# An attention and mixture-of-experts kernel: the expert stage's DMAs put in a fixed order per queue

## The chip, the cores and the metric

The kernel runs on one core of one Trainium2 chip. The metric is the device time of one launch in microseconds. The kernel before took 986.78 us, the median of 3 runs.

## What is computed

The reference is a chain of three layers on 3072 tokens of 384 numbers.

```python
# 1: linear attention with decay (batch 4, heads 8, sequence 768, head size 48)
state = alpha[:, :, t, :, None] * state + einsum('bhd,bhe->bhde', k[:, :, t], v[:, :, t])
y[:, :, t] = einsum('bhd,bhde->bhe', q[:, :, t], state)
# 2: a gated block (384 -> 1024 -> 1024 -> 384)
x = ((x @ w1) * (x @ w2) @ w3) @ w_out
# 3: 8 experts (384 -> 1024 -> 384), each token goes to the two with the largest logits
noisy_logits = x @ w_gate + log1p(exp(x @ w_noise)) * noise
out[mask] += top2_w * (maximum(x[mask] @ w1[e], 0) @ w2[e])
```

The change is in the third layer, the expert stage.

## The kernel before

**The stages.** Attention and the gated block run interleaved on TensorE until expert 0's first layer; the gated block's last products come last. The tokens go in 8 groups of 384 (three tiles of 128 rows). When the last narrow product of a group is done, `finish` (L566) scales its rows, cuts them into a high and a low float16 half ("xr") and stores them to a table of rows in device memory, "x2s" (L583). `route` (L607) then works out the two experts and the two factors of each token on VectorE. `rank` (L650) counts, with a product on TensorE of the 0/1 matrix "M" (L657), the place that each token gets in its experts' lists, and GpSimd writes number and factor there, six scattered writes a group (L686) into "table". The groups' rankings go one after another; the last one, `rank(NG - 1)`, comes inside expert 0's second layers.

**One expert.** An expert takes up to 832 tokens in two parts, 512 and 320 (the list `PARTS`, L949); what is over goes to a loop at the end (`overflow`). For a part, `fetch_part(e, p)` (L955) does three things: SP loads the part's slots from "table" into "mt" (`slots`, L939), and GpSimd gathers the rows of each 128 tokens from "x2s" into "xg" (`gather`, L883). `turn_part` (L963) then has SP transpose an "xg" into its place in "xT" by a DMA (`turn`, L890). Expert 0's and 1's first parts hold only tokens of the first six groups, so they don't need the last two rankings; their second parts need them. `first(e, p, f)` (L967, `layer1` L893) is one of eight steps of the first layer: nine matmuls (L897 to L899) into one bank, ScalarE's relu to "hh" (L900) and VectorE's rest "hl" (L901). `second(e, p, t)` (L973, `layer2` L903) makes 24 matmuls (L907 to L909) for 128 tokens, ScalarE scales the result into "ysb" (L930), and GpSimd adds it to the output by an indirect DMA (L931). The last 64 tokens of a part of 320 go through `last_few` (L981).

**The weights.** `expert_weights` (L826) and `weight_steps` (L840) give a list of small steps for each of the two matrices. A matrix is loaded in two halves, each by one DMA of SP into one of three buffers "es" (L853). VectorE takes each half's largest absolute value (L856), then "em", the larger of both for each partition (L859); TensorE's one-column product `over_all` takes it over the partitions (L864); five small steps make a scale of it (L868 to L872, "esc"); then ScalarE and VectorE cut the half into a high and a low float16 part, "eh" and "el" (L181 and L185, in `split`). A buffer is free for the next load when its half is cut. Below, the matrices are a (first) and b (second) and their halves a0, a1, b0 and b1.

**What sets the order.** These steps wait in a list, `todo`. `prepare(n)` (L1008) takes n of them, after a first, a second layer or a narrow product; the list `EARLY` says how many are taken behind each of the last narrow products. TensorE runs in the order of the code. The other engines' instructions are placed by a scheduler, which may move them past each other where no data forbids it and `tc.issue_after` does not say otherwise. SP's and GpSimd's DMAs are among these: each engine issues its own in the order in which they stand, and one that has to wait holds up what stands behind it.

```python
1022    def experts():
1023        leave(ST2)
1024        weights_for(1)
1025        fetch_part(1, 0)
1026        for f in range(NF):
1027            first(0, 0, f)
```

In the loop over the experts 1 to 7 (from L1058 on) TensorE's order is: first layer of part 0, first layer of part 1, four second layers of part 0, three of part 1. Expert 1's first layer of part 0 stands ahead of expert 0's of part 1.

Of the kernel before, what the change touches and what calls it, by code (L numbers as in the profile page):

```python
# [20 lines left out]
P = 128  # L21
# [3 lines left out]
E = 8  # L25
# [31 lines left out]
Q1 = 1  # L57
Q2 = 3
Q3 = 1
Q4 = 1  # L60
ST1 = 15
ST2 = 9
EARLY = (3, 3, 3, 3, 0, 0, 1, 0, 1, 0, 1, 0, 1, 0, 0, 0, 0, 0, 2, 0, 0, 0, 1, 1, 1, 1)
T1 = 1
# [21 lines left out]
def body(ctx, tc, q, k, v, alpha, mw1, mw2, mw3, mwo, wg, wn, noise, ew1, ew2, out, dbg=None):  # L86
# [564 lines left out]
    def rank(g):  # L651
# [32 lines left out]
        for j in range(2):  # L684
            for t in range(TG):
                i = nc.gpsimd.indirect_dma_start(  # L686
                    out=table_rows, out_offset=bass.IndirectOffsetOnAxis(ap=ad[:, j, t:t + 1], axis=0),
                    in_=md[:, j, t, :], in_offset=None)
# [134 lines left out]
    ep = None  # L823

    def expert_weights(e):
# [10 lines left out]
        if isinstance(e, int) and e == 0:  # L836
            return r, a[:2] + b[:1] + a[2:4] + b[2:3] + a[5:10] + b[1:2] + a[10:] + b[3:4] + b[5:]
        return r, a[:2] + b[:1] + a[2:-NK] + b[1:2] + a[-NK:] + b[2:]

    def weight_steps(src, e, n, m, hi, lo, sc):  # L840
# [8 lines left out]
        def get(i):  # L849
# [3 lines left out]
            nc.sync.dma_start(s[i], half(w, i))  # L853
# [29 lines left out]
    def gather(mt, t, rows=NTOK + P):  # L883
        xg = ep.tile([P, 2 * DM], F16, name="xg", bufs=7)
        nc.gpsimd.indirect_dma_start(  # L885
            out=xg, out_offset=None, in_=x2s[:rows],
            in_offset=bass.IndirectOffsetOnAxis(ap=mt[:, t, 0:1].bitcast(U32), axis=0))
        return xg

    def turn(xg, xT, t):  # L890
        nc.sync.dma_start_transpose(out=xT[:, :, t * P:(t + 1) * P], in_=xg)
# [36 lines left out]
    def put(py, n, mt, wv, t, e=None):  # L928
        ys = ep.tile([P, DM], F32, name="ysb", bufs=3)
        nc.scalar.activation(ys[:n], py, AF.Copy, scale=wv[:n, t:t + 1])  # L930
        i = nc.gpsimd.indirect_dma_start(  # L931
            out=out, out_offset=bass.IndirectOffsetOnAxis(ap=mt[:n, t, 0:1].bitcast(U32), axis=0),
            in_=ys[:n], in_offset=None, compute_op=OP.add)
# [85 lines left out]
    def leave(n):  # L1019
        prepare(max(0, len(todo) - n))  # L1020

    def experts():
        leave(ST2)
        weights_for(1)
        fetch_part(1, 0)
        for f in range(NF):
            first(0, 0, f)
            prepare(Q1)
        leave(ST1 + ST2)
        for t in range(NTP[0]):  # L1030
            turn_part(1, 0, t)
            second(0, 0, t)
            prepare(Q2)
            if t == 0:
                rank(NG - 1)
        fetch_part(0, 1)
        fetch_part(1, 1)
        leave(ST2)
        for f in range(NF):
            first(1, 0, f)  # L1040
            prepare(Q3)
            if 0 <= f - NF + NTP[1] + T1 < NTP[1]:
                turn_part(0, 1, f - NF + NTP[1] + T1)
        for f in range(NF):
            first(0, 1, f)
            prepare(Q4)
        leave(0)
        weights_for(2)
# [177 lines left out]
```

## Time and profile before

| | |
|---|---|
| median of 3 runs | 986.78 us (986.07 to 995.55) |
| the profiled execution | 993.42 us |
| its span | 991.7 us |
| mean granted clock of TensorE in it | 0.969 of full |
| TensorE, VectorE, ScalarE and GpSimd busy | 94, 62, 46 and 26% of the span |

All times of the trace are from the profiled execution, and count from the start of its span. A timeline row gives the start and the length of an instruction or a run of like ones, its engine, line and operation, what it writes and reads, how many they are (x), and in brackets the idle time of the engine before it with what ended that. L numbers are lines of the kernel before. Engines are PE (TensorE), PEld (its weight loads), DVE (VectorE), ACT (ScalarE), POOL (GpSimd) and SP; SPq is SP issuing a DMA. A windows row gives the busy time of PE, PEld, DVE, ACT and POOL in this order, each with its count of instructions, then the granted clock, the share of the DMA engines' time and the bytes moved.

### The profile page before, as it was taken

What the parts mean: (1) busy time and instruction counts of PE and PEld (TensorE: products, weight loads), DVE (VectorE), ACT (ScalarE), POOL (GpSimd) and SP (SyncE); (2) the same over time, 40 slices, a digit from 0 to 9 for tenths busy, and PEclk for the clock granted to TensorE, in tenths of its full rate; (3) what the DMA queues carried; (4) which work ended last, traced back from release to release, by engine and by line L of the source; (5) the groups of instructions that cost most, each with busy time, mean ns of one, the idle gap of its engine ahead of it and who ended that gap; (6) DMA issues with size and microseconds to landing.
All of it is one profiled execution on the core that took longest, in us unless ns stands there. A gap on an engine that the chain in (4) does not pass through costs nothing.

```text
span 991.7 us, 17686 instructions
## 1 busy us (share of the span) xinstructions
PE 927.8 (94%) x6823; PEld 607.9 (61%) x6823; DVE 615.6 (62%) x1697; ACT 457.6 (46%) x916; POOL 253.4 (26%) x246
## 2 busy tenths in 40 slices
PE   7889999999899998999979898999899999999996
PEld 4777777777566665766635454655456555655564
DVE  6698878676689696886657756525355453635220
ACT  3876764363555656555535342434233332433321
POOL 2121110004031403022222162333241424242313
PEclk9798999999999999999989998999899999999999
DMA  9895681406615033001051358567566475657203
GB/s 248 217 164 99 164 216 32 93 12 208 120 30 84 9 73 49 25 1 46 13 179 45 119 145 192 100 136 145 118 138 143 106 157 122 159 128 132 37 9 45
DMA packets 189269, 105.54 MB, mean 106 GB/s; under 512 B 156912, under 2 KB 174912, under 8 KB 189184
## 3 DMA queue, kind: packets, MB, share of 16 engines
q1 hardware_dynamic: 172624, 68.04, 30.7%
q0 software_dynamic: 16560, 36.37, 16.7%
q8 instruction: 54, 0.88, 0.4%
q14 instruction: 31, 0.25, 0.1%
HBM read 73.06 MB, written 20.31 MB: 94 GB/s over the span
## 4 chain that ended last, share of the span: by engine, by line
PE 55%; DVE 20%; issue 8%; ACT 7%; DMA 6%; SPq 3%; POOL 0%; POOLq 0%; ACTq 0%; DVEq 0%
PE ps L907 5%; PE ps L908 5%; PE ps L909 5%; PE ps L897 4%; PE ps L899 4%; PE ps L898 4%; DVE esc L856 3%; DMA es<-in_moe_w_dram 3%; PE ps L532 3%; PE ps L534 3%; PE ps L533 3%; PE ps L556 2%; PE ps L558 2%; PE ps L557 2%; PE ps L350 2%
## 5 line engine op out<-in xcount | busy, mean ns | idle before, releaser
L931 POOL DMA_INDIRECT out_dram<-ysb,mt x56 | 87.7, 1567 | 243.4 <-ACT ysb L930 141.0
L901 DVE SCALAR_TENSOR_TENSOR hl<-ps,hh 128x512 f16<-128x512 f32 (+1 forms) x128 | 74.4, 586 | 107.6 <-ACT hh L900 77.2
L897 PE MATMUL ps<-xT,eh 128*128 128x320 f16 (+1 forms) x384 | 131.9, 344 | 4.0 <-DMA xT<-xg 4.0
L898 PE MATMUL ps<-xT,eh 128*128 128x320 f16 (+1 forms) x384 | 132.2, 344 | 0.0
L899 PE MATMUL ps<-xT,el 128*128 128x320 f16 (+1 forms) x384 | 132.0, 344 | 0.0
L908 PE MATMUL ps<-el,hh 128*128 128x384 f16 x384 | 126.2, 329 | 0.0
L907 PE MATMUL ps<-eh,hh 128*128 128x384 f16 x384 | 126.1, 328 | 0.0
L909 PE MATMUL ps<-eh,hl 128*128 128x384 f16 x384 | 126.0, 328 | 0.0
L900 ACT ACTIVATE hh<-ps 128x512 f16<-128x512 f32 (+1 forms) x128 | 65.7, 515 | 110.4 <-PE ps L899 93.7
L930 ACT ACTIVATE ysb<-ps,wv 128x384 f32<-128x384 f32 (+1 forms) x56 | 32.4, 579 | 149.9 <-PE ps L909 103.4
L185 DVE SCALAR_TENSOR_TENSOR el<-es,esc,eh 128x512 f16<-128x512 f32 (+1 forms) x80 | 66.8, 855 | 46.6 <-ACT eh L181 41.4
L686 POOL DMA_INDIRECT table<-md,ad x48 | 49.5, 1031 | 147.9 <-DVE ad L683 102.8
L856 DVE TENSOR_REDUCE esc<-es 128x1 f32<-128x1536 f32 x32 | 55.9, 1746 | 38.8 <-DMA es<-in_moe_w_dram 35.2
L885 POOL DMA_INDIRECT xg<-x2s,mt x56 | 56.3, 1006 | 54.9 <-DMA mt<-table 32.1
L183 POOL TENSOR_TENSOR sm<-sf,sm 128x512 f16<-128x512 f32 x24 | 28.4, 1200 | 163.4 <-ACT sm L181 163.3
L532 PE MATMUL ps<-xT,w1h 128*128 128x384 f16 (+2 forms) x204 | 66.2, 325 | 2.0 <-ACT ab L536 1.6
L536 ACT ACTIVATE ab<-ps 128x384 f32<-128x384 f32 (+2 forms) x136 | 61.1, 465 | 14.9 <-PE ps L534 13.8
L556 PE MATMUL ps<-Wh,gh 128*128 128x400 f16 x192 | 64.8, 337 | 2.9 <-ACT gh L181 1.5
L181 ACT ACTIVATE eh<-es,esc 128x512 f16<-128x512 f32 (+1 forms) x80 | 61.9, 797 | 11.5 <-DVE esc L871 11.5
L534 PE MATMUL ps<-xT,w1l 128*128 128x384 f16 (+2 forms) x204 | 66.4, 326 | 0.0
L533 PE MATMUL ps<-xT,w1h 128*128 128x384 f16 (+2 forms) x204 | 66.4, 326 | 0.0
L532 PE MATMUL ps<-xT,w0h 128*128 128x384 f16 (+2 forms) x204 | 65.1, 320 | 1.1 <-ACT xT L403 1.1
(285 smaller groups left out, 2091.9 us busy)
## 6 DMA issues: line engine op xcount, KB each, us to landing
es<-in_moe_w_dram SPq DMA_DIRECT2D x32, 768.0 KB
s<-in_moe_w_dram POOLq DMA_DIRECT2D x16, 512.0 KB
out_dram<-zero POOLq DMA_DIRECT2D x5, 960.0 KB
v<-in_v_dram SPq DMA_DIRECT2D x24, 192.0 KB
x2s<-xr SPq DMA_DIRECT2D x24, 192.0 KB
pad<-in_alpha_dram SPq DMA_DIRECT2D x21, 192.0 KB
pad<-in_q_dram SPq DMA_DIRECT2D x21, 192.0 KB
pad<-in_k_dram SPq DMA_DIRECT2D x21, 192.0 KB
```

Source lines behind the costliest of these rows:

```text
L532: nc.tensor.matmul(pm, wab[i][0][:, kk, fs], xT[:, kk, cs], start=kk == 0, stop=False)
L533: nc.tensor.matmul(pm, wab[i][0][:, kk, fs], xT[:, NK + kk, cs], start=False, stop=False)
L534: nc.tensor.matmul(pm, wab[i][1][:, kk, fs], xT[:, kk, cs], start=False, stop=kk == NK - 1)
L556: nc.tensor.matmul(pm, gh[:, ts], Wf[0][:, f], start=f == 0, stop=False)
L856: nc.vector.tensor_reduce(sc[:, 5 + i:6 + i], s[i], AX.XY, OP.max, apply_absolute_value=True)
L897: nc.tensor.matmul(pm, w1h[:, kk, fs], xT[:, kk, :n], start=kk == 0, stop=False)
L898: nc.tensor.matmul(pm, w1h[:, kk, fs], xT[:, NK + kk, :n], start=False, stop=False)
L899: nc.tensor.matmul(pm, w1l[:, kk, fs], xT[:, kk, :n], start=False, stop=kk == NK - 1)
L907: nc.tensor.matmul(py[:n], hh[:, f, ts], w2h[:, f], start=f == 0, stop=False)
L908: nc.tensor.matmul(py[:n], hh[:, f, ts], w2l[:, f], start=False, stop=False)
L909: nc.tensor.matmul(py[:n], hl[:, f, ts], w2h[:, f], start=False, stop=f == NF - 1)
L931: i = nc.gpsimd.indirect_dma_start(out=out, out_offset=bass.IndirectOffsetOnAxis(ap=mt[:n, t, 0:1].bitcast(U32), axis=0), in_=ys[:n], in_o ...
```

## The change

All DMAs of the expert stage are made through a new function, `queued`, which holds each behind the one made last on either queue (SP's and GpSimd's): the order of the code is now the order of the queues. (Table writes are bound so only for the last group; in the overflow loop `line` is None and nothing is bound.) The code's order is changed with it. An expert's first three weight loads (a0, a1, b0) are made as soon as its list is opened, ahead of its slots; `next_weights(e + 2)` opens it behind the second layers of part 0 of expert e, where before it was opened at the start of expert e + 1. Its other steps are spaced by empty ones (`pause`), and both maxima of b stand next to each other. Expert 0's three loads stand ahead of the slot loads of expert 0 and 1. `rank(NG - 1)` moves from behind expert 0's first second layer to in front of it, and the slots and gathers of expert 0's second part from behind the four second layers to behind the first of them. In experts 2 to 7 the second part's slots are fetched ahead of the second layers of the expert before, and its transposes stand in these. There are three buffers for the slots of each part (two before) and eight for gathered rows (seven before).

```diff
-EARLY = (3, 3, 3, 3, 0, 0, 1, 0, 1, ...
+EARLY = (0, 3, 0, 3, 2, 1, 0, 1, 0, 1, ...
...
-                i = nc.gpsimd.indirect_dma_start(
+                i = queued(lambda: nc.gpsimd.indirect_dma_start(
                     out=table_rows, out_offset=bass.IndirectOffsetOnAxis(ap=ad[:, j, t:t + 1], axis=0),
-                    in_=md[:, j, t, :], in_offset=None)
+                    in_=md[:, j, t, :], in_offset=None), g > NG - NL)
...
+    line = {}
+
+    def queued(dma, on=True):
+
+        if not on or line is None:
+            return dma()
+        with ExitStack() as st:
+            for d in line.values():
+                st.enter_context(tc.issue_after(d))
+            d = dma()
+        line[d.ins.engine] = d.ins
+        return d
...
-        if isinstance(e, int) and e == 0:
-            return r, a[:2] + b[:1] + a[2:4] + b[2:3] + a[5:10] + b[1:2] + a[10:] + b[3:4] + b[5:]
-        return r, a[:2] + b[:1] + a[2:-NK] + b[1:2] + a[-NK:] + b[2:]
+        return r, a, b
...
-            nc.sync.dma_start(s[i], half(w, i))
+            queued(lambda: nc.sync.dma_start(s[i], half(w, i)))
...
-        xg = ep.tile([P, 2 * DM], F16, name="xg", bufs=7)
+        xg = ep.tile([P, 2 * DM], F16, name="xg", bufs=8)
...
-        mt = ep.tile([P, NTA, 2], F32, name=f"mt{part}")
-        nc.sync.dma_start(mt[:, :n], src)
+        mt = ep.tile([P, NTA, 2], F32, name=f"mt{part}", bufs=3)
+        queued(lambda: nc.sync.dma_start(mt[:, :n], src))
...
-        weights_for(0)
-    def begin_experts():
-        fetch_part(0, 0)
+        a, b = weights_for(0)
+        todo.extend(a[2:4] + b[2:3] + a[5:10] + b[1:2] + a[10:] + b[3:4] + b[5:])
+        for e in range(NFR):
+            fetch_part(e, 0)
...
     def weights_for(e):
-        EW[e], st = expert_weights(e)
-        todo.extend(st)
+        EW[e], a, b = expert_weights(e)
+        for get in a[:2] + b[:1]:
+            get()
+        return a, b
+    def pause(n):
+        return [lambda: None] * n
+    def next_weights(e):
+        a, b = weights_for(e)
+        todo.extend(pause(1) + a[2:4] + pause(1) + a[5:10] + b[1:2] + a[10:] + pause(1) + b[2:4] + pause(2) + b[5:])
...
     def experts():
-        leave(ST2)
-        weights_for(1)
-        fetch_part(1, 0)
+        prepare(len(todo))
+        a, b = weights_for(1)
+        todo.extend(pause(1) + a[2:4] + pause(1) + a[5:11] + b[1:2] + a[11:] + b[2:3] + pause(2) + b[3:4] + pause(1) + b[5:])
         for f in range(NF):
             first(0, 0, f)
-            prepare(Q1)
-        leave(ST1 + ST2)
+            prepare(1)
+        rank(NG - 1)
         for t in range(NTP[0]):
             turn_part(1, 0, t)
             second(0, 0, t)
-            prepare(Q2)
+            prepare(3)
             if t == 0:
-                rank(NG - 1)
-        fetch_part(0, 1)
-        fetch_part(1, 1)
-        leave(ST2)
+                fetch_part(0, 1)
         for f in range(NF):
             first(1, 0, f)
-            prepare(Q3)
-            if 0 <= f - NF + NTP[1] + T1 < NTP[1]:
-                turn_part(0, 1, f - NF + NTP[1] + T1)
+            prepare(1)
+            if 0 < f <= NTP[1]:
+                turn_part(0, 1, f - 1)
+        prepare(len(todo))
+        fetch_part(1, 1)
+        next_weights(2)
         for f in range(NF):
             first(0, 1, f)
-            prepare(Q4)
-        leave(0)
-        weights_for(2)
+            prepare(f // 4)
...
         for e in range(1, E):
-            if 1 < e < E - 1:
-                weights_for(e + 1)
             if e > 1:
-                fetch_part(e, 1)
...
-                    if 3 <= f < 3 + NTP[1]:
-                        turn_part(e, 1, f - 3)
             if e + 1 < E:
                 fetch_part(e + 1, 0)
...
+            if e + 1 < E:
+                fetch_part(e + 1, 1)
             for t in range(NTP[0]):
                 second(e, 0, t)
                 prepare(2)
                 if e + 1 < E:
                     turn_part(e + 1, 0, t)
             prepare(len(todo))
+            if e + 2 < E:
+                next_weights(e + 2)
             if e < E - 1:
                 for t in range(NTP[1] - 1):
+                    turn_part(e + 1, 1, t)
                     second(e, 1, t)
+                turn_part(e + 1, 1, NTP[1] - 1)
                 rest = last_few(e)
...
-        begin_experts()
```

In the three places below, rows of the two kernels' instruction orders are shown. A row is one instruction, or several in a row (x); L numbers are lines of the kernel it belongs to, those of the changed one being up to 10 larger or smaller than those given above, and a number in a tile's name tells buffers apart.

SP's DMAs around expert 0's first loads, before. "mt_6556" holds the slots of expert 0's first part; "es" of 3x512 is a half of a, of 4x384 a half of b.

```order
L853 DMA es<-in_moe_w_dram 128x3x512
L941 DMA mt_6556<-table 128x8
L853 DMA es<-in_moe_w_dram 128x3x512
L853 DMA es<-in_moe_w_dram 128x4x384
L891 DMA_TRANSPOSE xT_6558<-xg 128x6x128 x4
L853 DMA es<-in_moe_w_dram 128x4x384
```

The same place in the changed kernel ("mt_6562" and "mt_6573" hold the slots of expert 0's and 1's first parts, "xr" the rows of the last group):

```order
L856 DMA es<-in_moe_w_dram 128x3x512 x2
L856 DMA es<-in_moe_w_dram 128x4x384
L944 DMA mt_6562<-table 128x8
L944 DMA mt_6573<-table 128x8
L576 DMA x2s<-xr 128x768 x3
L856 DMA es<-in_moe_w_dram 128x4x384
L894 DMA_TRANSPOSE xT_6564<-xg 128x6x128 x4
```

Before, the second and third loads stood behind the slot load; now three loads stand in front of it, and expert 1's slot load behind it.

SP's DMAs beside expert 0's second layers and expert 1's first layer, before ("xT_7207" is expert 1's first part, "mt_7499" and "xT_7501" expert 0's second part, "mt_7508" the slots of expert 1's second part):

```order
L891 DMA_TRANSPOSE xT_7207<-xg 128x6x128 x4
L853 DMA es<-in_moe_w_dram 128x4x384
L941 DMA mt_7499<-table 128x6
L941 DMA mt_7508<-table 128x6
L853 DMA es<-in_moe_w_dram 128x3x512
L891 DMA_TRANSPOSE xT_7501<-xg 128x6x128 x3
```

The same place in the changed kernel ("xT_6575" is expert 1's first part, "mt_7397" and "xT_7399" expert 0's second part, "mt_7617" the slots of expert 1's second part):

```order
L894 DMA_TRANSPOSE xT_6575<-xg 128x6x128
L856 DMA es<-in_moe_w_dram 128x4x384
L944 DMA mt_7397<-table 128x6
L894 DMA_TRANSPOSE xT_6575<-xg 128x6x128 x3
L894 DMA_TRANSPOSE xT_7399<-xg 128x6x128 x3
L944 DMA mt_7617<-table 128x6
```

Three of the four transposes for expert 1's first layer now stand behind the slot load of expert 0's second part, which reads what the last ranking wrote.

VectorE beside expert 0's first layer, before. "hl" is that layer's own work, one row a step; "esc" and "em" are expert 1's maxima; L626 to L635 are the last group's routing.

```order
L901 SCALAR_TENSOR_TENSOR hl_7217<-ps,hh_7216 128x512
L629 TENSOR_REDUCE rr<-ln 128x3
L856 TENSOR_REDUCE esc_7199<-es 128x1
L630 TENSOR_TENSOR oh<-rev,rr 128x24
L901 SCALAR_TENSOR_TENSOR hl_7217<-ps,hh_7216 128x512
L632 SCALAR_TENSOR_TENSOR nl<-oh,nl 128x24
L856 TENSOR_REDUCE esc_7199<-es 128x1
L626 TENSOR_REDUCE m<-nl 128x3
L901 SCALAR_TENSOR_TENSOR hl_7217<-ps,hh_7216 128x512
L627 TENSOR_TENSOR ln<-nl,m 128x24
L635 TENSOR_TENSOR w<-m 128x3
L859 TENSOR_REDUCE em<-esc_7199 128x1
```

The same layer in the changed kernel, from its second step on (L178 is the cut of the last group's third tile of rows, L590 to L593 an earlier part of the routing):

```order
L904 SCALAR_TENSOR_TENSOR hl_7223<-ps,hh_7222 128x512
L178 SCALAR_TENSOR_TENSOR xr<-x_7039,am,xr 128x384
L590 TENSOR_SCALAR lg_7157<-lg_7156 128x24
L859 TENSOR_REDUCE esc_7210<-es 128x1
L592 SCALAR_TENSOR_TENSOR lg_7157<-lg_7157,lg_7156 128x24
L904 SCALAR_TENSOR_TENSOR hl_7223<-ps,hh_7222 128x512
L592 SCALAR_TENSOR_TENSOR lg_7157<-lg_7157,lg_7156 128x24
L859 TENSOR_REDUCE esc_7210<-es 128x1
L592 SCALAR_TENSOR_TENSOR lg_7157<-lg_7157,lg_7156 128x24
L904 SCALAR_TENSOR_TENSOR hl_7223<-ps,hh_7222 128x512
L593 SCALAR_TENSOR_TENSOR lg_7157<-lg_7157,lg_7155 128x24
L862 TENSOR_REDUCE em<-esc_7210 128x1
```

Both maxima and "em" stand two steps earlier in the layer, in front of most of the last group's routing.

## Rows read from the trace of the kernel before

**Rows 1.** the page, section 1: busy us (share of the span), instructions

```profile
PE 927.8 (94%) x6823; PEld 607.9 (61%) x6823; DVE 615.6 (62%) x1697; ACT 457.6 (46%) x916; POOL 253.4 (26%) x246
```

**Rows 2.** TensorE's waits from 480 us on: us in total, times, longest

```profile
PE ps L864 <- DVE em L859: 18.9, 10, 7.0
```

**Rows 3.** timeline of TensorE at waits: start, us, instruction [idle before <-releaser]

```profile
482.90 1.10 PE L339 MATMUL ps<-Zs,Qt 112*128 112x96 f32 x8 [1.98 <-DVE Zs L394]
505.96 0.16 PE L864 MATMUL ps<-em,part 128*128 128x1 bf16 x1 [6.97 <-DVE em L859]
564.50 0.18 PE L864 MATMUL ps<-em,part 128*128 128x1 bf16 x1 [3.03 <-DVE em L859]
603.57 0.43 PE L897 MATMUL ps<-xT,eh 128*128 128x320 f16 x1 [4.02 <-DMA xT<-xg]
700.12 0.16 PE L864 MATMUL ps<-em,part 128*128 128x1 bf16 x1 [4.53 <-DVE em L859]
808.02 0.16 PE L864 MATMUL ps<-em,part 128*128 128x1 bf16 x1 [1.76 <-DVE em L859]
```

**Rows 4.** windows behind them: length, busy by engine, PEclk, DMA share, GB/s

```profile
505.96:510.10 4.14, 4.14 (x14) 1.96 (x14) 3.27 (x8) 1.68 (x3) 0.19 (x1) 0.50 0.76 212
564.50:568.10 3.60, 3.60 (x10) 1.34 (x11) 2.26 (x17) 0.12 (x1) 0.00 (x0) 0.53 0.00 0
603.57:609.10 5.53, 5.53 (x21) 3.14 (x22) 3.71 (x4) 0.87 (x2) 3.57 (x4) 0.50 0.92 326
700.12:704.65 4.53, 4.53 (x16) 2.17 (x16) 1.16 (x7) 0.00 (x0) 0.18 (x1) 0.50 0.59 167
808.02:812.00 3.98, 3.98 (x26) 2.42 (x26) 1.17 (x7) 0.00 (x0) 1.58 (x1) 1.00 0.89 234
```

**Rows 5.** timeline of SP's DMA issues (SPq) before expert 0

```profile
498.91 0.33 SPq L941 DMA_DIRECT2D mt<-table  x1
```

**Rows 6.** chain of work that ended last, 498 to 505

```profile
499.33 4.61 DMA es<-in_moe_w_dram
```

**Rows 7.** timeline of VectorE (DVE) at expert 0's maxima

```profile
503.96 1.75 DVE L856 TENSOR_REDUCE esc<-es 128x1 f32<-128x1536 f32 x1 [9.42 <-DMA es<-in_moe_w_dram]
```

**Rows 8.** timeline of TensorE: expert 0's layers and the last ranking

```profile
547.71 0.38 PE L897 MATMUL ps<-xT,eh 128*128 128x512 f16 x1
568.16 0.33 PE L907 MATMUL ps<-eh,hh 128*128 128x384 f16 x1
572.07 0.18 PE L657 MATMUL ps<-M,before 128*128 128x24 bf16 x1
```

**Rows 9.** timeline of VectorE beside expert 0's first layer

```profile
554.97 0.62 DVE L185 SCALAR_TENSOR_TENSOR xr<-x,am,xr 128x384 f16<-128x384 f32 x1 [1.27 <-ACT xr L181]
556.46 0.68 DVE L901 SCALAR_TENSOR_TENSOR hl<-ps,hh 128x512 f16<-128x512 f32 x1
564.30 0.14 DVE L859 TENSOR_REDUCE em<-esc 128x1 bf16<-128x2 f32 x1
566.32 0.17 DVE L647 CAST M<-R 128x8 bf16<-128x8 f32 x1
```

**Rows 10.** timeline of GpSimd (POOL): the last ranking's first table write

```profile
576.40 1.00 POOL L686 DMA_INDIRECT table<-md,ad  x1 [1.64 <-DVE ad L683]
```

**Rows 11.** timeline of SP behind them: slot loads, expert 0's transposes

```profile
585.47 0.81 SPq L941 DMA_DIRECT2D mt<-table  x2
594.50 4.04 SPq L891 DMA_TRANSPOSE xT<-xg  x3
```

**Rows 12.** chain of work that ended last, 594 to 605

```profile
597.19 6.24 DMA xT<-xg
```

**Rows 13.** timeline of VectorE: the maxima of a second matrix, a later expert

```profile
803.30 1.75 DVE L856 TENSOR_REDUCE esc<-es 128x1 f32<-128x1536 f32 x1 [4.46 <-DMA es<-in_moe_w_dram]
```

**Rows 14.** the page, section 5: gathers; xcount, busy us, mean ns, idle before

```profile
L885 POOL DMA_INDIRECT xg<-x2s,mt x56 | 56.3, 1006 | 54.9 <-DMA mt<-table 32.1
```

**Rows 15.** timeline of SP: transposes of a second part behind a weight load

```profile
687.83 7.70 SPq L891 DMA_TRANSPOSE xT<-xg  x3
```

More of the change, by code (lines that the diff above doesn't have):

```diff
@@ L56 @@
 R2 = 1.9
[L57 to L64, printed above, removed]
+EARLY = (0, 3, 0, 3, 2, 1, 0, 1, 0, 1, 0, 1, 0, 1, 0, 0, 0, 0, 2, 0, 1, 1, 1, 1, 0, 0, 0, 0)
 PGL = range(4)
@@ L883, in gather @@
     def gather(mt, t, rows=NTOK + P):
-        xg = ep.tile([P, 2 * DM], F16, name="xg", bufs=7)
-        nc.gpsimd.indirect_dma_start(
+        xg = ep.tile([P, 2 * DM], F16, name="xg", bufs=8)
+        queued(lambda: nc.gpsimd.indirect_dma_start(
             out=xg, out_offset=None, in_=x2s[:rows],
-            in_offset=bass.IndirectOffsetOnAxis(ap=mt[:, t, 0:1].bitcast(U32), axis=0))
+            in_offset=bass.IndirectOffsetOnAxis(ap=mt[:, t, 0:1].bitcast(U32), axis=0)))
         return xg
     def turn(xg, xT, t):
-        nc.sync.dma_start_transpose(out=xT[:, :, t * P:(t + 1) * P], in_=xg)
+        queued(lambda: nc.sync.dma_start_transpose(out=xT[:, :, t * P:(t + 1) * P], in_=xg))
     def layer1(f, w1h, w1l, xT, n, hh, hl):
@@ L930, in put @@
         nc.scalar.activation(ys[:n], py, AF.Copy, scale=wv[:n, t:t + 1])
-        i = nc.gpsimd.indirect_dma_start(
+        i = queued(lambda: nc.gpsimd.indirect_dma_start(
             out=out, out_offset=bass.IndirectOffsetOnAxis(ap=mt[:n, t, 0:1].bitcast(U32), axis=0),
-            in_=ys[:n], in_offset=None, compute_op=OP.add)
+            in_=ys[:n], in_offset=None, compute_op=OP.add))
         if e in (0, E - 1):
@@ L1017, in prepare @@
                 todo.pop(0)()
-    def leave(n):
-        prepare(max(0, len(todo) - n))
     def experts():
-        leave(ST2)
-        weights_for(1)
-        fetch_part(1, 0)
+        prepare(len(todo))
+        a, b = weights_for(1)
+        todo.extend(pause(1) + a[2:4] + pause(1) + a[5:11] + b[1:2] + a[11:] + b[2:3] + pause(2) + b[3:4] + pause(1) + b[5:])
         for f in range(NF):
             first(0, 0, f)
-            prepare(Q1)
-        leave(ST1 + ST2)
+            prepare(1)
+        rank(NG - 1)
         for t in range(NTP[0]):
@@ L1054, in experts @@
         rest = last_few(0)
-        prepare(2)
         li = overflow_plan()
         for e in range(1, E):
-            if 1 < e < E - 1:
-                weights_for(e + 1)
             if e > 1:
-                fetch_part(e, 1)
                 for f in range(NF):
@@ L1125, in overflow @@
     def overflow(li):
+        nonlocal line
+        line = None
         total = nc.values_load(li[0:1, 2, 0:1], min_val=0, max_val=NOV)
@@ L1129, in overflow @@
             t = nc.sync.value_load(li[0:1, 1, bass.ds(j, 1)], min_val=OVF // P, max_val=TCOLS - 1)
-            (w1h, w1l, s1, w2h, w2l, s2), steps = expert_weights(e)
-            for step in steps:
+            (w1h, w1l, s1, w2h, w2l, s2), a, b = expert_weights(e)
+            for step in a[:2] + b[:1] + a[2:-NK] + b[1:2] + a[-NK:] + b[2:]:
                 step()
```

## Prediction

> **What bounds the kernel now.** I read the page's busy times first, then TensorE's waits from 480 us on, its timeline at each wait, the granted clock behind each, and the queues that feed them. TensorE is busy for 94% of the span [rows 1], so only its idle time and its slow time can be won, unless matmuls go, and this change takes none away. In the part that the change touches (from 480 us on), the one matmul behind "em", which averages an expert's largest weights over the partitions, waited ten times for VectorE, 18.9 us in total [rows 2]. The timeline has the large ones: 6.97, 3.03, 4.53 and 1.76 us, and a 4.02 us wait for transposed tokens [rows 3]; the other six small waits for "em" make 18.9 - 16.3 = 2.6 us, of which 1.79 is one more of the kind of 1.76, two experts on, and the rest five of 0.16. The 1.98 us at 482.90 is in the attention part, which does not move.
>
> After the waits of 3 us and more the granted clock was 0.50 to 0.53 of full, the 1.2 GHz level, for 4.14, 3.60, 5.53 and 4.53 us; behind the wait of 1.76 us it stayed at 1.00 [rows 4]. Half speed loses half of such a stretch: 2.07, 1.80, 2.77 and 2.27 us. So the stage holds 22.1 us of waits (6.97 + 3.03 + 4.02 + 4.53 + 1.76 + 1.79) and 8.9 us of slow clock, 31.0 us in all. That is the most that can be won.
>
> **Part 1, expert 0's loads in front of its slots: -9.0 us.** Before, SP came to the slot load "mt" only at 498.91, as that needs the last table entries of a ranking, and two weight loads stood behind it [rows 5]. One took 4.61 us to land [rows 6]; VectorE idled 9.42 us for it [rows 7], TensorE 6.97. Now three weight loads stand ahead of the slots. The second needs only the last attention matmul that reads a certain buffer, the form that started at 482.90 [rows 3], so it is issued at about 484 and lands by 489 with a load of 4.61. VectorE, which took its first maximum at about 493 in front of that gap, can take the second at once: two of 1.75 us [rows 7] give "em" by about 497. TensorE comes to it one part later than before, near 501. Cover 4 us. The wait and its clock loss go: 6.97 + 2.07 = 9.04. What is late next: the load of the fourth half waits for cuts that now fall into the busy stretch before the last narrow product. It could cost 0 to 1.5 us there; I take nothing, and keep the 1.5 for the range.
>
> **Part 2, the first layer of expert 0 and the last ranking.** I count from N, the start of that layer (547.71 before [rows 8]). One of its eight steps takes (564.50 - 3.03 - 547.71) / 7 = 1.97 us. Expert 1's "em" matmul moves from behind step 7 to behind step 5, that is from N + 13.8 to N + 9.8, and its two maxima move as much in VectorE's order. But VectorE is the late one here: it does the last group's routing between them. It ended the third row split at 555.59 = N + 7.9, after 1.27 us idle for ScalarE [rows 9]. Behind that it now has two maxima (3.5), two products of 0.68 [rows 9], four routing steps (about 0.2 each by the M row [rows 9]) and "em" (0.14): N + 13.7, a wait of 3.9 us. If the split comes earlier, since the weight cuts now end before the layer and the stores of the split rows share the DMAs with fewer loads, it is at most those 1.27 us and some 0.5 more: a wait of 2.1. I take 3.0, no gain, with its clock loss of 1.8. The layer then ends at N + 9.8 + 3.0 + 5.9 + 1.8 = N + 20.5, as before (568.16 = N + 20.45 [rows 8]).
>
> The ranking now stands in front of the second layers, and its matmul needs M. Before, M was whole at 566.49 = N + 18.8 [rows 9]; the new order puts one more cut and five scale steps in front, about 1.5 us: N + 20.3, in time (at worst 0.8 late). So the ranking starts at N + 20.5, against 572.07 = N + 24.4 before [rows 8]: one tile of 3.91 us earlier.
>
> **Part 3, transposes for expert 1 behind a slot load: a new wait.** Before, all four stood ahead of the slots. Now three stand behind the slot load of expert 0's second part, which needs the ranking's six table writes. From ranking to first write took 4.33 us, from there to the slot load 9.07 [rows 8, 10, 11]: 13.4 after the ranking. Then 0.41 for its issue, and three transposes of 1.35 us each [rows 11]; the last starts 3.1 us behind the load. How long it takes from there to land: 1.35 at least, 6.24 at most, where weights, gathers and table writes crowded it [rows 12]. Here only output adds run beside it, so I take 2.2, near the lower end. Data at 13.4 + 3.1 + 2.2 = 18.7 us behind the ranking; TensorE comes after four tiles, 15.7. New wait: 3.0 us (2.2 to 7.0), and 1.8 us of slow clock. Expert 1's first layer starts at N + 39.2 instead of N + 36.1 (599.55 less eight steps). It ends at N + 54.9 and by then the tokens for expert 0's second part are long there, as their gathers run beside it. Before, that part started at 603.57 = N + 55.9 with 2.77 us of slow clock to come. Sum of parts 2 and 3: -0.9 - 2.8 + 1.8 = -1.9 us.
>
> **Part 4, experts 2 to 7: -10.3 us.** Before, an expert's first loads were asked for at the start of the expert before it, the fourth behind the transposes of a second part; 803.30 is VectorE waiting 4.46 us for it [rows 13]. And the scheduler had put the maximum of that late half ahead of the maximum of the half that was there. Now three loads are asked for while the second layers before run, the fourth two steps into a second part, with nothing but a small slot load in front; both maxima stand at the end of that part, and their matmul behind two more tiles (7.8 us), for 2 x 1.75 us of VectorE work. So 4.53 + 2.27 + 1.76 + 1.79 = 10.35 go. The 0.16 us waits stay, as both maxima of the first matrix keep their distance of two steps to the matmul.
>
> **Edits at no cost.** The third slot buffer: no row shows a wait for the second. POOL's line: seven gathers of 1.01 us [rows 14] now stand ahead of an expert's output adds. They end about one tile into the second layers, and three output buffers of 3.91 us each cover it; without that cover ScalarE, then TensorE, would wait for the rest.
>
> **Sum.** 9.0 + 1.9 + 10.3 = 21.2 us off the profiled execution's 993.42 (its span of 991.7 and 1.7 around it) gives 972.2. That execution is 6.6 us above the median of 986.78, and none of the waits used is known to be larger in it, so I take them off the median: 965.6 us.
>
> **Rivals.**
> *New waits at full price.* The wait of part 2 is 3.9, M comes 0.8 late, the transposes take 6.24 (4 us more), and the fourth half of expert 0 costs 1.5. That is 0.9 + 0.8 + 4.0 + 1.5 = 7.2 us: 972.8. For it: VectorE has no idle time in that stretch but the 1.27. Against: nothing as large as the weight loads moves beside these transposes.
> *The order is not what made them late.* If the waits of experts 2 to 7 come from VectorE's own line (maxima behind cuts and products) and not from the loads, fixing the loads leaves them: 965.6 + 10.3 = 975.9, and with part 3 at its top end 980. Against it: VectorE idled for the loads in front of both, 4.46 us in one of them [rows 13].
> *Slower: transposes behind three weight loads.* For each next expert's second part, the three transposes now stand on SP behind three loads, the last of which waits for the last cut, about 2 us behind the four tiles: 17.7 us after these begin. Load 4.61, issue 7.70, the slowest seen, beside a weight load [rows 15], landing 6.24: 36.3. They are needed after 15.7 + 7.8 + 15.7 = 39.2. Spare: 3 us. If they land later than that, each us costs six, once for each of experts 2 to 7; from 42.7 on the gain of 21 us is gone, and 5.3 us late in each gives 965.6 + 32 = 997.6. The row of 7.70 against 4.04 for three [rows 11] speaks for it; that all prices must be at the top and more speaks against. The Trainium skill (DMA: Bandwidth & Descriptors, section Queues, rings and completion order) says that each DMA engine takes the descriptors of one ring in order, so a transpose issued behind weights on SP cannot pass them; by that rule the case is possible at every expert, and the two issue times agree with it.
>
> **How the numbers follow.** The forecast has 0.60 and its own range, 958 to 971: without both new waits and their slow clock (3.0 + 1.8 + 3.0 + 1.8 = 9.6) it would be 956.0, of which I leave off 2 us; upwards, three quarters of the first rival's 7.2. The first rival has 0.22, the second 0.12, the third 0.04, and 0.02 is for more than all listed. The floor is 986.78 - 31.0 = 955.8, the low end 956; the high end 979 takes in the first rival and most of the second. A measurement of this kernel tells about 1% from no change: 976.9 is that bound. Faster by more: 0.60 + 0.20 of the first + 0.05 of the second + 0.02 = 0.87. Within: 0.02 of the first, 0.06 of the second, 0.01 of the third, 0.09. Slower: 0.01 of the second and 0.03 of the third, 0.04.
>
> **What would show it.** Right: no wait for "em" near 500; one of 2 to 4 us behind step 5 of expert 0's first layer; a wait for transposed tokens of 2 to 7 us at expert 1's first layer and none at expert 0's second part; no wait over 0.5 us for "em" in experts 2 to 7, and no slow clock after about 600. Wrong: waits for transposes in every expert, or VectorE's maxima still idle in front of loads.

## The result and the profile after

The changed kernel takes 975.2 us, the median of 4 runs (972.08 to 978.31). The kernel before, with one run more beside it, has a median of 990.09 (986.07 to 995.55). The ratio is 0.9853, with a 95% interval of 0.9817 to 0.9889: 14.6 us less (0.0147 of 990.09), where 21.2 was forecast. The profiled execution took 978.31 us against 993.42 before, 15.1 less.

TensorE's busy time [rows 1] now stands in this row of the page:

```profile
PE 924.2 (95%) x6823; PEld 607.8 (62%) x6823; DVE 616.1 (63%) x1697; ACT 457.8 (47%) x916; POOL 254.0 (26%) x246
```

TensorE's waits in the changed kernel from 480 us on (us in total, times, longest). The first row answers to [rows 2]: 18.9 us have become 6.4.

```profile
PE ps L867 <- DVE em L862: 6.4, 7, 2.4
PE ps L900 <- DMA xT<-xg: 4.5, 1, 4.5
PE ps L332 <- DVE Zs L387: 2.0, 1, 2.0
PE ps L651 <- DVE M L640: 0.5, 1, 0.5
```

The timeline of TensorE at these waits, to be read against [rows 3], and the windows behind them, against [rows 4]:

```profile
524.95 0.18 PE L867 MATMUL ps<-em,part 128*128 128x1 bf16 x1 [1.61 <-DVE em L862]
553.13 0.18 PE L867 MATMUL ps<-em,part 128*128 128x1 bf16 x1 [1.60 <-DVE em L862]
559.67 0.17 PE L651 MATMUL ps<-M,ones 128*128 128x24 bf16 x1 [0.50 <-DVE M L640]
579.97 0.58 PE L900 MATMUL ps<-xT,eh 128*128 128x512 f16 x1 [4.51 <-DMA xT<-xg]
666.65 0.16 PE L867 MATMUL ps<-em,part 128*128 128x1 bf16 x1 [2.38 <-DVE em L862]
```

```profile
483.00:486.50 3.50, 3.50 (x36) 2.65 (x36) 1.16 (x5) 1.44 (x4) 0.00 (x0) 0.51 0.36 60
553.13:557.00 3.87, 3.87 (x19) 1.80 (x20) 3.49 (x19) 0.67 (x2) 0.00 (x0) 1.00 0.01 2
579.97:585.43 5.46, 5.46 (x13) 1.87 (x14) 0.00 (x0) 1.42 (x2) 3.54 (x3) 0.50 1.12 186
666.65:670.76 4.11, 4.11 (x13) 1.55 (x13) 0.59 (x2) 0.60 (x1) 0.85 (x1) 0.58 0.40 48
```

The reader is to see four things. The wait of 6.97 near 500 is gone, and one of 1.61 stands at the em product of expert 0's second matrix. Expert 1's em product waits 1.60 at full clock, where it waited 3.03 and then ran at 0.53. The wait for transposed tokens moved from expert 0's second part to expert 1's first layer and is no smaller: 4.51, and half of 5.46 at clock 0.50, 7.2 us. And one wait of 2.38 with its slow clock (0.42 of 4.11, 1.7) stands in experts 2 to 7, in place of 4.53, 1.76 and 1.79.

By parts: part 1 gave 9.04 - 1.61 = 7.4; parts 2 and 3 4.83 + 6.79 - 1.60 - 0.50 - 7.24 = 2.3; part 4 10.35 - 2.38 - 1.7 = 6.2. The attention wait of 2.0 us that both kernels have cost 1.7 of clock this time (0.51 in the first window). That is 14.2 of the 15.1.

### The profile page after: what moved, and what is told of

Same layout as the page of the kernel before. It is cut to its first block, busy times and chain, and to the rows that moved or that the text cites. A ratio compares the mean times of both kernels' runs of the same rounds, so it can differ in the third digit from the quotient of the medians.

```text
span 976.6 us, 17652 instructions
## 1 busy us (share of the span) xinstructions
PE 924.2 (95%) x6823; PEld 607.8 (62%) x6823; DVE 616.1 (63%) x1697; ACT 457.8 (47%) x916; POOL 254.0 (26%) x246
## 5 line engine op out<-in xcount | busy, mean ns | idle before, releaser
L178 DVE SCALAR_TENSOR_TENSOR el<-es,esc,eh 128x512 f16<-128x512 f32 (+1 forms) x80 | 67.0, 856 | 46.4 <-ACT eh L174 45.1
L525 PE MATMUL ps<-xT,w0h 128*128 128x384 f16 (+2 forms) x204 | 65.4, 322 | 1.1 <-ACT xT L396 1.1
L526 PE MATMUL ps<-xT,w0h 128*128 128x384 f16 (+2 forms) x204 | 65.4, 322 | 0.0
L527 PE MATMUL ps<-xT,w0l 128*128 128x384 f16 (+2 forms) x204 | 65.3, 321 | 0.0
```

Source lines behind the costliest of these rows:

```text
L178: nc.vector.scalar_tensor_tensor(lo, src, scale, hi, op0=OP.mult, op1=OP.subtract)
L525: nc.tensor.matmul(pm, wab[i][0][:, kk, fs], xT[:, kk, cs], start=kk == 0, stop=False)
L526: nc.tensor.matmul(pm, wab[i][0][:, kk, fs], xT[:, NK + kk, cs], start=False, stop=False)
L527: nc.tensor.matmul(pm, wab[i][1][:, kk, fs], xT[:, kk, cs], start=False, stop=kk == NK - 1)
```

## The experiments

Each ratio is to the kernel before on the same chip, with its 95% interval. Times of the trace are of one profiled execution. The fourteen traces reach TensorE's wait of 2.0 us in the attention part between 480.50 and 487.82 us, and only the first weight load of all that the edits touch lies ahead of it. So where a trace is compared as a whole below, it is from the end of that wait to the end of the span ("the rest"): 508.8 us before, 494.0 in the changed kernel (1.7 of these are slow clock behind that wait; the trace of before has none there).

**Part 1 undone (slots_between).**

```diff
-        a, b = weights_for(0)
+        EW[0], a, b = expert_weights(0)
+        a[0]()
+        fetch_part(0, 0)
+        for get in a[1:2] + b[:1]:
+            get()
...
-        for e in range(NFR):
-            fetch_part(e, 0)
+        fetch_part(1, 0)
```

> The changed kernel with part 1 undone: expert 0's slot load stands behind its first weight load again, and the other two behind it. Theory (SP blocked by the slot load made the wait near 500): a wait for em of 5 to 7 us near 505 with 2 us of slow clock, and 982 to 984. Rival (by now the wait would move to the next em or be hidden by the new spacing of steps): less than 4 us over 975.

Measured 980.95 us, 0.989 (0.9869 to 0.9911). TensorE waits at 509.31:

```profile
509.31 0.19 PE L867 MATMUL ps<-em,part 128*128 128x1 bf16 x1 [4.97 <-DVE em L862]
```

The wait is back, just under the low end of what was expected; the time rose by less, 3.7 us by the ratios (0.989 against 0.9853), whose intervals overlap. The rest took 495.4 us, 1.4 more than in the changed kernel: other waits were shorter in this execution (1.24 at the next em product, 0.63 at the one of 2.38). So the cause of the wait is shown, but not that removing it is worth 7 us in the new order.

**Part 1 alone, on the kernel before (loads_first_on_before).**

```diff
+        prepare(3)
         fetch_part(0, 0)
```

> The kernel before, with one thing moved: expert 0's first three weight loads are made ahead of its slot load. Theory (part 1 stands by itself): the wait of 6.97 us for em near 506 and the 2.07 us of slow clock behind it go, less up to 1.6 us of wait for the fourth half: 7.4 to 9.0 us less than before, 981 to 983 where before is 990, and every later wait of before is there still. Rival (the wait is VectorE's own, or comes back at the next em): less than 4 us gained.

Measured 998.36 us, 1.0056 (1.0032 to 1.0079): slower. The wait near 506 is gone, but the next em product waits 13.21 us. The edit had a second effect: with three steps taken from the list, all later ones came up, and this product with them. So the same again with three empty steps in their place.

**Part 1 alone, the list kept (loads_first_same_steps).**

```diff
+        prepare(3)
+        todo[:0] = [lambda: None] * 3
         fetch_part(0, 0)
```

> The kernel before with expert 0's first three weight loads ahead of its slot load, as in the earlier run of this kind, but with three empty steps in front of the list, so that every other step keeps its place (in that run all later steps moved up by three, and the product for em of the second matrix came some ten narrow products too early, which is one cause for its wait of 13.2 us). Theory (part 1 stands by itself, the earlier loss was the moved list): no wait for em over 2 us before 540, and 6 to 9 us less than before, 982 to 984. Rival (the fourth load, behind four transposes on SP, is late all the same): a wait for em of 4 us or more near 530, and less than 4 us gained.

Measured 989.53 us, 0.9973 (0.9933 to 1.0012): neither. No em product waits before 563, but the median shows no gain clear of noise (the rest of this trace took 504.5 us against 508.8 before). TensorE now waits for M, the matrix of the ranking before the last:

```profile
526.63 0.20 PE L657 MATMUL ps<-M,before 128*128 128x24 bf16 x1 [3.60 <-DVE M L645]
527.82 0.18 PE L658 MATMUL ps<-M,ones 128*128 128x24 bf16 x1 [0.98 <-DVE M L647]
```

The timelines of ScalarE and of SP show why:

```profile
520.02 0.61 ACT L181 ACTIVATE xr<-x,am 128x384 f16<-128x384 f32 x1 [8.00 <-DMA x2s<-xr]
```

```profile
501.32 0.34 SPq L941 DMA_DIRECT2D mt<-table  x1
507.05 7.19 SPq L891 DMA_TRANSPOSE xT<-xg  x4
514.33 0.54 SPq L853 DMA_DIRECT2D es<-in_moe_w_dram  x1
514.96 6.67 SPq L583 DMA_DIRECT2D x2s<-xr  x3
```

ScalarE's third split of a group's rows waited 8.00 us for an "xr" buffer, whose store stood on SP behind four transposes; VectorE's routing, and so M, stood behind that split. The two waits and the slow clock behind them, 3.60 + 0.98 + 2.7, took back 7.3 of the 9.0. In the changed kernel the stores stand ahead of the transposes. Part 1 needs that as well.

**The transposes in front of the slot load (turns_first).**

```diff
         for t in range(NTP[0]):
             turn_part(1, 0, t)
+        for t in range(NTP[0]):
             second(0, 0, t)
```

> The changed kernel, but all four transposes for expert 1's first layer stand in front of the slot load of expert 0's second part. Theory (three of them wait for that slot load, which waits for the last ranking's table writes): the wait of 4.51 us at expert 1's first layer and the 2.7 us of slow clock behind it go, some 7 us less than the changed kernel's 975.2, about 968, and no new wait over 1 us at expert 0's second part, as its three transposes still have the 15.7 us of expert 1's first layer. Rival (the transposes are late by their own issue and landing, in a crowd of gathers and table writes): the wait stays at 3 us or more and the time within 2 us of 975.2. Second rival (the wait only moves on to expert 0's second part): a wait of 3 us or more for transposed tokens there, and less than half of the 7 us gained.

Measured 974.26 us, 0.9813 (0.9777 to 0.985). No matmul waits for transposed tokens any more, at either place, so the slot load in front was the cause and both rivals fall:

```profile
PE ps L867 <- DVE em L862: 5.9, 7, 3.5
PE ps L332 <- DVE Zs L387: 2.0, 1, 2.0
PE ps L651 <- DVE M L640: 1.3, 2, 0.8
```

By the ratios it is 4.0 us less than the changed kernel, not 7, and the intervals overlap. The rest took 487.1 us, 6.9 less than in the changed kernel, although the em product of expert 0's second matrix waited longer:

```profile
530.99 0.19 PE L867 MATMUL ps<-em,part 128*128 128x1 bf16 x1 [3.46 <-DVE em L862]
```

**The ranking one tile later (rank_back).**

```diff
-        rank(NG - 1)
         for t in range(NTP[0]):
...
             if t == 0:
+                rank(NG - 1)
                 fetch_part(0, 1)
```

> The changed kernel with the last ranking behind the first second layer again, the slot load of expert 0's second part right behind it. Theory (the chain ranking, table writes, slot load, transposes sets the start of expert 1's first layer): all of it comes one tile, 3.9 us, later, the wait for transposed tokens there grows from 4.5 to about 8.4 us, less the 0.5 us wait for M that goes, and the time is 978 to 980. Rival (the slot load waits for something else, such as its queue): the wait stays within 1 us of 4.5.

Measured 976.94 us, 0.9869 (0.9846 to 0.9892). The first row of TensorE's waits:

```profile
PE ps L900 <- DMA xT<-xg: 7.7, 1, 7.7
```

3.2 us more than in the changed kernel, and the wait for M is gone: the chain from the ranking sets this wait (one tile, 3.9, was expected). The time itself rose by 1.6 us, within what the intervals can't tell.

**Part 4 undone (late_experts).** The loop over the experts from 2 on, and the places of their weights, are those of before; the queues stay in the order of the code, and the extra buffers stay.

```diff
-        next_weights(2)
...
+            if 1 < e < E - 1:
+                weights_late(e + 1)
             if e > 1:
+                fetch_part(e, 1)
...
+                    if 3 <= f < 3 + NTP[1]:
+                        turn_part(e, 1, f - 3)
```

> The changed kernel with part 4 undone: from expert 2's weights on, loads, maxima, slots and transposes stand in the code where they stood before, still in a fixed order per queue. Theory (part 4 is worth the 6 to 10 us that the traces of before and after differ by from 610 us on): 981 to 985, with waits for em of 1.5 to 4.5 us in experts 2 and later again, and ScalarE's waits for output adds, 28.7 us in the changed kernel, under 10 us, as fewer gathers stand in front of the adds. Rival (the fixed order alone cures these waits, wherever the loads stand): 975 within 2 us.

Measured 989.87 us, 0.9999 (0.9976 to 1.0022): the whole gain is gone. But the waits are others than expected:

```profile
PE ps L900 <- DMA xT<-xg: 20.1, 8, 5.7
PE ps L867 <- DVE em L862: 3.9, 7, 1.6
```

Em is in time without the new places, as the rival had it, though in part because TensorE comes later: it waits 1.25 us for transposes at 731.46, and its next em product, at 749.04, comes 0.7 us after em is there. Now the second parts' transposes are late, once in each of experts 1 to 7; the eighth wait, 3.30, is the one at expert 1's first part that the changed kernel has too. SP's timeline at the worst of them, a wait of 5.74 us ended at 622.15:

```profile
606.54 1.22 SPq L894 DMA_TRANSPOSE xT<-xg  x1
607.86 1.06 SPq L856 DMA_DIRECT2D es<-in_moe_w_dram  x2
609.01 1.46 SPq L894 DMA_TRANSPOSE xT<-xg  x1
610.52 0.57 SPq L856 DMA_DIRECT2D es<-in_moe_w_dram  x1
611.14 4.18 SPq L894 DMA_TRANSPOSE xT<-xg  x1
```

The last transpose was issued behind three weight loads, and took 4.18 us to issue against 1.22 for the first. It landed at 622.11, just behind the load in front of it (621.54). A fixed order is only as good as the order: with the new places both em and these transposes are in time, but for the one wait of 2.38. The Trainium skill (DMA: Bandwidth & Descriptors, section Queues, rings and completion order) says that each DMA engine takes up the descriptors of a ring in ring order; the two landings agree with it, in another kernel than the one for which the prediction weighed it. The same sentence adds that a later transfer may finish its write before an earlier one, so the prediction's "cannot pass them" goes further than the page; here the transpose did land second. The two issue times that the prediction names tell how long SP took, not the order inside a ring.

**The output adds made independent (adds_free).**

```diff
-        if e in (0, E - 1):
+        if e is not None:
```

> The changed kernel, but within every expert the output adds are declared independent of each other, as they were for experts 0 and 7 only. Theory (in experts 1 to 6 each add waits for the one before it to land, 5.1 us apart against 3.9 us that TensorE takes for a tile; as they now begin behind seven gathers, ScalarE runs out of its three output buffers and its relu comes late): ScalarE's nine waits for output adds, 28.7 us, fall under 8 us, the wait of 2.38 us for em near 667 and its 1.7 us of slow clock go, and the time is about 971, 4 us under 975.2. Rival (em near 667 is late because VectorE gets its weights late): that wait stays at 2 us or more, and the time at 975 within 2 us.

Measured 980.18 us, 0.9885 (0.9845 to 0.9926). What it was to cure stands in the changed kernel's waits of ScalarE, and in its timeline of GpSimd:

```profile
ACT ysb L933 <- DMA out_dram<-ysb,mt: 28.7, 9, 5.6
```

```profile
655.76 1.56 POOL L934 DMA_INDIRECT out_dram<-ysb,mt  x1 [4.56 <-ACT ysb L933]
660.88 1.55 POOL L934 DMA_INDIRECT out_dram<-ysb,mt  x1 [3.56 <-ACT ysb L933]
665.93 1.56 POOL L934 DMA_INDIRECT out_dram<-ysb,mt  x1 [3.50 <-issue]
```

Adds stand 5.1 us apart there, each behind the landing of the one before (4.3 us after its issue, the median of the trace), slower than the 3.91 us of a tile. The wait of 2.38 for em at 666.65 comes from this: ScalarE waits for a landing, and VectorE's "hl", which stands ahead of the maxima, waits for ScalarE:

```profile
660.24 0.58 ACT L933 ACTIVATE ysb<-ps,wv 64x384 f32<-64x384 f32 x1 [3.82 <-DMA out_dram<-ysb,mt]
661.33 0.69 DVE L904 SCALAR_TENSOR_TENSOR hl<-ps,hh 128x512 f16<-128x512 f32 x1 [4.19 <-ACT hh L903]
```

With the edit the adds stand 3.9 apart, ScalarE's waits for them are 9.0 us (still over the 8 expected), and the em products of experts 2 to 7 wait 0.16 each, as the theory has it; but the median shows no gain. The rest took 490.1 us, 2.9 less than in the next run, the changed kernel once more, and neither has slow clock behind the attention wait; so what the edit is worth stays open. The next run says what became of the wait of 2.38.

**The changed kernel once more (as_changed).** No edit.

> The changed kernel itself, once more, as a control. Theory (the wait of 2.38 us for em near 667 belongs to that one execution, as four kernels with the same experts have 0.16 to 0.63 there): 0.2 to 0.7 us there, the waits of 1.60 at expert 1's em and of 3.3 to 4.6 for transposed tokens again, and a ratio to before of 0.983 to 0.988. Rival (it belongs to the kernel): 2 us or more there again.

Measured 978.79 us, 0.9869 (0.9821 to 0.9917). TensorE's timeline:

```profile
532.39 0.18 PE L867 MATMUL ps<-em,part 128*128 128x1 bf16 x1 [3.49 <-DVE em L862]
562.15 0.18 PE L867 MATMUL ps<-em,part 128*128 128x1 bf16 x1 [1.60 <-DVE em L862]
587.65 0.38 PE L900 MATMUL ps<-xT,eh 128*128 128x512 f16 x1 [3.18 <-DMA xT<-xg]
670.65 0.16 PE L867 MATMUL ps<-em,part 128*128 128x1 bf16 x1 [0.20 <-DVE em L862]
```

The wait of 2.38 was that execution's own (ScalarE's waits for adds were 15.8 us here instead of 28.7); the em product of expert 0's second matrix waited 3.49 here instead of 1.61, with 1.7 of slow clock. The losses from there on wander, their sum hardly: some 16 us in each, and the rest took 493.0 us against 494.0. What made this execution 3.3 us longer than the other (981.57 against 978.31) lies ahead of the expert stage: it came to the attention wait at 486.79 us, the other at 482.56.

**Two slot buffers (mt2).**

```diff
-        mt = ep.tile([P, NTA, 2], F32, name=f"mt{part}", bufs=3)
+        mt = ep.tile([P, NTA, 2], F32, name=f"mt{part}")
```

> The changed kernel with two buffers for the slots of each part, as before, where it has three. Theory (no slot load waits for a buffer: costs nothing): the same time as the changed kernel within 2 us, slot loads at the same places. Rival (in a fixed order a slot load that waits for a buffer holds up the weights and transposes behind it): new waits for em or transposed tokens, 3 us or more.

Measured 985.83 us, 0.9958 (0.9923 to 0.9992), against 0.9869 for the changed kernel on the same chip: 8.8 us slower, and the intervals don't overlap. The rival holds, though in several small waits: em waits 11.5 us in total where the control has 6.9, with two of 2.35 us. SP's waits from 600 to 960 us have a row that the changed kernel's have not:

```profile
SPq L944 <- DMA out_dram<-ysb,mt: 30.9, 6, 8.4
```

The adds read their rows from the slots, so a buffer is free when its expert's last add has landed; with two buffers SP waits for that at the slot load, and the gathers and transposes behind it with it.

**No DMA held behind another (unpinned).**

```diff
-    line = {}
+    line = None
```

> The changed kernel with all its moves in the code, but no DMA is held behind another: the scheduler places them again. Theory (the gain needs the fixed order, as the scheduler puts slot loads that must wait in front of weight loads and transposes, here four slot loads in a row behind the last ranking): new waits for em or for transposed tokens, 3 to 10 us in total, 978 to 985. Rival (the order of the code does it, the pinning nothing): 975 within 2 us, or 968 to 970, as all four transposes for expert 1 are ahead of the slot load in this order.

Measured 1014.44 us, 1.0237 (1.0196 to 1.0278), worse than expected. Its em products wait 12.2 us in total, and no matmul waits for transposed tokens. The scheduler put slot loads of experts 1 and 2 in a row behind that of expert 0's second part, and on GpSimd their gathers ahead of expert 0's last adds. The windows of this kernel ahead of expert 1's first layer and in it:

```profile
564.00:586.00 22.00, 21.48 (x126) 11.81 (x124) 14.46 (x53) 7.35 (x13) 10.80 (x10) 1.00 0.47 94
586.00:601.00 15.00, 10.06 (x41) 3.44 (x38) 3.11 (x9) 2.04 (x4) 10.93 (x11) 1.00 1.05 233
```

**Two em products later (later_products),** on top of turns_first.

```diff
-EARLY = (0, 3, ..., 0, 0, 0, 0, 2, 0, 1, 1, 1, 1, 0, 0, 0, 0)
+EARLY = (0, 3, ..., 0, 0, 0, 0, 0, 2, 1, 1, 1, 1, 0, 0, 0, 0)
...
-        todo.extend(pause(1) + a[2:4] + pause(1) + a[5:11] + b[1:2] + a[11:] + ...
+        todo.extend(pause(1) + a[2:4] + pause(2) + a[5:10] + b[1:2] + a[10:] + ...
```

> All four transposes of expert 1 in front of the slot load, as in the run that had only this, and the em products of expert 0's second matrix and expert 1's first matrix each one unit of TensorE work (about 2 us) later. Theory (these two products came too early for VectorE, by 3.46 and 1.60 us in that run, and their scales are not needed soon): both waits fall by 1.6 to 2 us each, no other wait comes, and the ratio to before is about 0.977, 3 to 4 us under that run. Rival (the later cuts of these weights are waited for in turn): a new wait for eh or el, or a later M, and no gain.

Measured 966.42 us, 0.9763 (0.9738 to 0.9788), with the ratio that was expected: it beats both kernels, though its interval still meets that of turns_first. The two em waits are gone, but "no other wait comes" was wrong: one of 1.5 us for "gh" in the gated block came. Its waits from 480 us on:

```profile
PE ps L332 <- DVE Zs L387: 2.0, 1, 2.0
PE ps L867 <- DVE em L862: 1.7, 5, 0.8
PE ps L549 <- ACT gh L174: 1.5, 1, 1.5
PE ps L650 <- DVE M L638: 0.8, 1, 0.8
PE ps L651 <- DVE M L640: 0.7, 1, 0.7
```

**The same with the adds independent (later_free):** the edit of adds_free on later_products.

> The version with the four transposes in front and the two em products later, and besides the output adds of every expert declared independent. Theory (ScalarE's 20 us of waits for output adds cost TensorE about 1 us in that version): ratio to before 0.975 to 0.977. Rival (adds that don't wait for each other crowd the DMA engines and delay weights and transposes): 0.978 or more, with new waits.

Measured 971.3 us, 0.9801 (0.9763 to 0.984). ScalarE's waits for adds fell from 20.0 us to 3.2, and the time did not. The rest took 482.9 us against 482.5 in later_products, 1.7 of the latter slow clock behind the attention wait. That these waits cost TensorE anything lasting is not shown; that independent adds harm is not either, as the intervals overlap.

## Why the prediction was right, and where its sizes were off

The direction and the mechanism hold: idle TensorE in front of em and of transposed tokens was what could be won, and most of it went. The time lies inside the range, 9.6 us above the forecast. About 3.3 us of that is the median taken for the kernel before: three runs gave 986.78, four 990.09. The rest is in the terms.

- **Part 1, -9.0.** The wait and its clock loss went, and no wait near 500 came back. "I take nothing" for the fourth half was the mis-sized term: the profiled execution had 1.61, the control 3.49 with 1.7 of slow clock, and all nine profiled executions with this product in its place, these two among them, had 1.24 to 3.78. Undone in the changed kernel, the part is worth 3.7 us by the ratios, within the noise. Nor does it stand alone: on the kernel before it measured 0.9973, which can't be told from no change, as a store behind transposes became the wait.
- **Part 2, new wait 3.0 and 1.8 of clock.** The wait is 1.60, in every run that had it within 0.01, and the clock stayed at 1.00. The layer starts at 541.65 now and the third split ends at 548.04, 6.4 us into it instead of 7.9: the earlier split that the lower bound of 2.1 was made from, and the wait went 0.5 below it.
- **Part 3, new wait 3.0 and 1.8.** Measured 4.51 and 2.7, the control 3.18 and 1.7. The mechanism is shown by turns_first and rank_back. The place of the slot load was right (first table write to slot load 9.1 us, as before), the landing behind it was not:

```profile
572.35 0.33 SPq L944 DMA_DIRECT2D mt<-table  x1
572.77 10.90 SPq L894 DMA_TRANSPOSE xT<-xg  x6
```

  From the slot load to 579.97 are 7.6 us, where 5.3 was taken. The three transposes for expert 1 were issued 1.35 us apart, as taken; the third, issued at 575.47, landed at 579.83, 4.4 us later, where 2.2 was taken: this is the mis-sized term. "Only output adds run beside it" was wrong; GpSimd's timeline has three gathers there, this the first:

```profile
574.97 1.00 POOL L888 DMA_INDIRECT xg<-x2s,mt  x1 [1.89 <-issue]
```

  Parts 2 and 3 together came out at 2.3 for 1.9: what part 2 saved, 1.4 of wait and 1.8 of clock, paid for what part 3, with M's 0.5, cost more. That the sum fits is luck.
- **Part 4, -10.3.** The named waits went. That fixing the loads alone would do it is not borne out: late_experts has no em wait over 0.2 us there with the fixed order and the old places, in part because TensorE comes later, and what the new places do is to keep the transposes from being late. The price that was missed is GpSimd's: "three output buffers of 3.91 us each cover it" took adds at TensorE's pace, and they go at 5.1 us. In the profiled execution that led to the wait of 2.38 and cost 4.1 with its clock; in the control all em waits of experts 2 to 7 together are 1.8 us, and the clock stayed up.
- **Edits at no cost.** "No row shows a wait for the second" buffer was read from the old order, in which slots were fetched later. In the new one the third buffer carries 8.8 us of the gain. The eighth buffer for gathered rows was not varied. The step that failed is to price a resource by the waits of an order that the change replaces.
- **Rivals.** By the number the second, 975.9, came nearest to 975.2, but by luck: the waits of experts 2 to 7 that it keeps went. By its terms the first did, 972.8: M came 0.5 late, the fourth half cost 1.61 and the transposes landed 2.3 later than taken, while the wait of part 2 was 1.60 and not 3.9. The slower one, transposes behind three loads, did not come in the changed kernel, but is what part 4 undone runs into.

Left open: how the terms of one execution go over into a median. The sum of the two traces holds to 1 us, yet single losses of 2 to 5 us differ between executions of one kernel, and the part ahead of the expert stage alone differs by up to 7.3 us between the fourteen traces, so a difference of a few us between medians of four runs says little of the stage.

## What to carry to other kernels

Holding DMAs in the order of the code gained nothing here while the experts from 2 on kept their old places (0.9999), and the new places without it were slower than before (1.0237): the order has to be written for it, each load ahead of whatever waits on a late producer, and each slot, store and transpose has to be looked at on its queue. Before counting a buffer as free, work out who reads it last in the new order. And when steps are taken from a list that paces other work, fill their places, or the experiment measures the shift.

## What the runs showed of the hardware

- The same wait of 2.0 us in the attention part was followed by clock 0.51 in the changed kernel's window above, and by 1.00 in the trace of before:

```profile
482.90:486.50 3.60, 3.60 (x45) 2.82 (x46) 1.79 (x7) 1.91 (x5) 0.00 (x0) 1.00 0.00 0
```

  In ten of the fourteen traces it was half clock, in four full clock. Two waits of 2.35 us for em in mt2 show the same: 1.00 behind the one that ended at 677.17, 0.51 behind the one that ended at 836.22. Behind the nine waits of 1.6 us for expert 1's em the clock stayed at 1.00; behind all those for transposed tokens at its first layer (3.2 to 7.7 us) it stood at the 1.2 GHz level. The attention wait of 2.0 us costs 2.0 or 3.7.
- In the kernel without fixed order TensorE was idle for a third of 15 us (10.06 of 15.00 above) at full clock, between matmuls that waited for nothing that the profile shows, while the DMA engines were busy throughout (1.05). What held it is not known. Traffic alone is not shown to be the cause: in the changed kernel's window above with a share of 1.12 TensorE, at half clock, was busy throughout. No transfer of an instruction queue falls into these 15 us.
